# Gate rows from column products and a DRAM broadcast, value runs in single steps, the second key half summed on VectorE, transposes evacuated in pairs

## The chip, the core and the metric

The kernel runs on one core of one Trainium2 chip. Times are device microseconds; the time of the kernel before is the median of four runs, 1138.79 us (1138.46 to 1139.82). A profile is one execution, recorded by the hardware. It names TensorE "PE" (its weight loads "PEld"), VectorE "DVE", ScalarE "ACT", GpSimd "POOL" and SyncE "SP"; lines such as L960 are lines of the kernel's source.

## What is computed

One transformer block with adaptive layer norm, for 2048 tokens of width 1024, all in bf16:

```python
mod = (_silu(c) @ w_mod).reshape(c.shape[0], 6, 1, -1)
sa, ca, ga, sb, cb, gb = (mod[:, i] for i in range(6))
h = _layernorm(x) * (1 + ca) + sa
# 32 query heads of width 32, one key head and one value head (wk, wv: 1024 x 32)
q = h @ wq ; k = h @ wk ; v = h @ wv
p = softmax(q k^T / sqrt(32))            # per head, 2048 x 2048
x = x + ga * ((p v) @ wo)
h = _layernorm(x) * (1 + cb) + sb
x = x + gb * ((silu(h @ w1) * (h @ w3)) @ w2)     # w1, w3: 1024 x 3584
```

The vectors ga and gb ("gates") scale the columns of the attention's and of the MLP's output.

## The kernel before

**Who orders the work.** The program is written as a graph (class Dag). Every `G.add` names an engine, what the instruction reads and writes, an estimated duration and a priority. `schedule` runs through this graph with the estimates and fixes the order of the instructions on each engine; `emit` writes them in this order, with the waits that the data needs. An engine therefore works in the order found when the program was built, whatever the real durations are. At the places where several kinds of instruction could go next, `choose` may take another than the one the priorities prefer; the table CH (line 17) lists these decisions by the number of the choice. Two of the eight PSUM banks (PB0, PB1) go round among groups of matmuls; the other six (SP) hold scores during attention and join the round before and after.

**The head.** SyncE loads x, the first two parts of w_mod, and wq. The vector silu(c) lies as a column tile SCT (128 x 8). The first two modulation vectors are products of 128 x 128 weight tiles with single columns of SCT (L759), eight per load. LayerNorm statistics run on VectorE and for two tiles on ScalarE; TensorE transposes the normalized tiles (L624), and `ln_transpose` copies each transposed 128 x 512 piece out of PSUM, on ScalarE (L635) or VectorE (L638). Then follow the key projection (`kproj`, L674), the value projection (L690) and the query projection (`qproj`, L700), the last one for the first 256 tokens; the other query projections are filler for later.

**Attention.** It works on blocks of 256 queries, eight in all, and in each on eight groups f of four heads. One `step` takes two key tiles: eight score products (L960, four heads side by side), then two exps of 128 x 1024 on ScalarE (L970) into one of eleven U buffers. There are 64 steps per block, 512 in all. `finish` multiplies the U buffers of one f with V (L1026, 64 products of 256 columns, four heads side by side), in runs of two steps at a time. The sum of the exps over the keys (the softmax's denominator) is made in part by VectorE, which adds U buffers into a tree buffer (L987, L993; L1003 folds two of them), and then by products of the tree buffer with a selector of ones (L1053). The ratio is made from L1065, L1074, L1077 (evictions), L1083 (reciprocal), L1088 (spread) and L1093 (multiplication).

In block 0 the first four groups (HEAD = 4) run through the first half of the keys (h = 0) before the second half (h = 1), since later keys aren't projected yet. For the halves in DIRECT = (0, 1), that is both, VectorE makes no sum: four U buffers go straight to the selector products, 32 per half and group. L1062 adds the second half's result.

**After attention.** `post` does the output projection (L1158) with wo, whose columns were scaled by ga on VectorE (L895, 8 instructions), adds x (L1162), normalizes and transposes (through TensorE in the first and last block, with a transposing DMA, L1169, in the others). The MLP runs as 448 products of 256 columns for w1 and w3 (L1199) per block, tanh on ScalarE (L1207), three VectorE instructions (L1204, L1214, L1219), then the second layer (L1270, 224 products of 256 columns; L1241 in the last block). The MLP of one block is the filler between the score products of the next block. The weights w1, w3 and w2 come again for each block, through a ring of six buffers: three in WREG (behind WQ and the gates' weights), two in HREG, one in X.

**The gates before.** Four 128 x 4 x 512 pieces of w_mod per gate are loaded into three WMS slots. GpSimd spreads SCT into eight 128 x 128 tiles whose columns are all equal (SCB, L558). A product of such a tile with 512 columns of w_mod puts the gate's row on all 128 partitions at once (L884, sixteen products of 512 columns per gate), and L888 copies it into GBB, twice per gate. The modulation vectors 3 and 4 are made as in the head, by single columns (L910).

Of the kernel before, what the change touches and what calls it, by code (L numbers as in the profile page):

```python
# [16 lines left out]
CH = {88: 2, 187: 1, 188: 1, 196: 1, 205: 1, 224: 1, 229: 1, 262: 1, 329: 2, 352: 1, 362: 1, 375: 1, 411: 1,  # L17
      442: 1, 609: 2, 654: 2, 662: 1, 731: 1, 775: 1, 851: 2, 1272: 1, 1290: 2, 1463: 1, 1478: 1, 1492: 1, 1497: 1,
      1526: 1, 1897: 1, 1915: 2, 2088: 1, 2103: 1, 2117: 1, 2122: 1, 2151: 1, 2522: 1, 2540: 2, 2713: 1, 2728: 1,
      2742: 1, 2747: 1, 2776: 1, 3147: 1, 3165: 2, 3338: 1, 3353: 1, 3367: 1, 3372: 1, 3401: 1, 3772: 1, 3790: 2,  # L20
      3963: 1, 3978: 1, 3992: 1, 3997: 1, 4009: 1, 4163: 1, 4339: 1, 4342: 1, 4490: 1}
# [15 lines left out]
class Dag:  # L37
# [77 lines left out]
    def choose(self, t, e, n, alts):  # L115
        self.nch += 1
        return CH.get(self.nch - 1, 0)

# [295 lines left out]
def build(nc, x_in, wq_in, wk_in, wv_in, wo_in, w1_in, w3_in, w2_in, c_in, wmod_in, out, S, D, F):  # L414
# [41 lines left out]
    ACTP = -1  # L456
    TP = -1
# [9 lines left out]
    SCT = sb("SCT", [P, NC], BF16)  # L467
    CROW = sb("CROW", [8, P], BF16)
# [26 lines left out]
    DIRECT = (0, 1)  # L495
# [3 lines left out]
    SCB = [QT[:, k // 4, S - 512 + (k % 4) * P:S - 512 + (k % 4 + 1) * P] for k in range(NC)]  # L499
    WKV = QT[:, NC - 1, S - 512:S].rearrange("p (a c f) -> p a c f", a=2, c=NC)  # L500
    WKK, WVK = [("QT", NC - 1, S - 512), ("QT", NC - 1, S - 384)], [("QT", NC - 1, S - 256), ("QT", NC - 1, S - 128)]
    SCBK = [("QT", a, S - 512 + b) for a in range(NC // 4) for b in range(0, 512, P)]
# [14 lines left out]
    def grp(allow=None):  # L517
        g = Group()
        g.allow = allow
        return g  # L520
# [36 lines left out]
    for a in range(NC // 4):  # L557
        G.add("pool", lambda e, a=a: e.tensor_copy(  # L558
            QT[:, a, S - 512:S].rearrange("p (k q) -> p k q", q=P),
            SCT[:, a * 4:a * 4 + 4].unsqueeze(2).broadcast_to([P, 4, P])), reads=["SCT"],  # L560
            writes=[("QT", a, S - 512 + b) for b in range(0, 512, P)], dur=0.6)
# [52 lines left out]
    def ln_transpose(nt, q0, dst, dkeys, fs, fm, engs, prio=5, cbs=None, allow=None, bp=0):  # L614
# [3 lines left out]
        for cb in range(NC // ncb) if cbs is None else cbs:  # L618
            g = grp(allow)
            for i in range(nt):  # L620
                def tr(e, i=i, g=g, cb=cb):
                    for h in range(ncb):
                        c = cb * ncb + h
                        r = e.transpose(PBH[g.bank][:, h * w + i * P:h * w + (i + 1) * P],  # L624
                                        xnt(q0 + i)[:, c * P:(c + 1) * P], IDENT[:])
                    return r
                G.add("pe", tr, reads=["IDENT"] + [k for j in (range(nt) if i == 0 else (i,)) for k in [("XN", q0 + j)] + xnk(q0 + j)], dur=ncb * 0.065, lat=0.2,
                      acq=g if i == 0 else None, groups=[(g, "w")], mode="F", prio=prio)
            for h in range(ncb):
# [81 lines left out]
    ONPOOL = ()  # L711
    KP = 1
# [158 lines left out]
    def gate(m, scale):  # L871

        for h in range(2):
            g = grp()
            for kb in range(2):
# [6 lines left out]

                for k in range(4):
                    G.add("pe", lambda e, kb=kb, k=k, sl=sl, g=g: e.matmul(  # L884
                        PB[g.bank], SCB[kb * 4 + k], WMS[:, sl, k, :], start=(kb == 0 and k == 0),
                        stop=(kb == 1 and k == 3)), reads=SCBK + wms(sl), dur=MM, lat=0.2,
                        acq=g if kb == 0 and k == 0 else None, groups=[(g, "w")], mode="F")
            G.add("dve", lambda e, g=g, h=h: e.tensor_scalar(GBB[:, h * 512:(h + 1) * 512], PB[g.bank], scale, None,  # L888
                                                             ALU.mult),
                  writes=[("GBB", h)], groups=[(g, "r")], dur=dve_t(512), prio=4)  # L890

    G.chain = GCH
    gate(2, 1.0)
    for f in range(NC):
        G.add("dve", lambda e, f=f: e.tensor_tensor(WO[:, f, :], WO[:, f, :], GBB[:], ALU.mult),  # L895
              reads=["WO", ("GBB", 0), ("GBB", 1)], writes=[("WOG", f)], dur=dve_t(1024, 2), prio=6)
    for m in range(2):
        g = grp()
        for h in range(2):
            for kb in range(2):  # L900
                sl = nwm[0] % 3
                nwm[0] += 1
                c0 = (3 + m) * D + h * 512
                dma(lambda e, kb=kb, c0=c0, sl=sl: e.dma_start(
                    WMS[:, sl], wmod_in[kb * 512:(kb + 1) * 512, c0:c0 + 512].rearrange("(c p) f -> p c f", p=P)),
                    ("wms", sl), writes=wms(sl), nbytes=P * 2048 * 2)
# [10 lines left out]
        a, b2 = ((1.0, 0.0), (1.0, 1.0))[m]  # L917
        G.add("dve", lambda e, g=g, m=m, a=a, b2=b2: e.tensor_scalar(
            MODC[:, 3 + m, :], PB[g.bank][:, 0:8], a, b2, ALU.mult, ALU.add),
            writes=[("MODC", 3 + m)], groups=[(g, "r")], dur=0.15, prio=4)  # L920
    gate(5, 0.5)
# [9 lines left out]
    def attention(q0, qn):  # L931
# [65 lines left out]
        def finish(f, h=None):  # L997
# [21 lines left out]
            for w0 in range(0, nn, 2):  # L1019
                part = pend[w0:w0 + 2]  # L1020
# [43 lines left out]
            else:  # L1064
                G.add("dve", lambda e, g=g, f=f: e.tensor_copy(ASB[:, f % 4, 0:qn], PB[g.bank][:, 0:qn]),  # L1065
                      writes=[("ASB", f % 4), ("XN", 2 + f % 4 // 2)], groups=[(g, "r")], dur=dve_t(qn), prio=1)
# [5 lines left out]
            if ga not in opened:  # L1072
                opened.add(ga)
                G.add("dve", lambda e, g=g, da=da: e.tensor_copy(DSB[:, da, 0:qn], PB[g.bank][:, qn:2 * qn]),  # L1074
                      writes=[("DSB", da)], groups=[(g, "r")], dur=dve_t(qn), prio=1)
# [283 lines left out]
```

## Time and profile before

| | us |
|---|---|
| median of four runs | 1138.79 |
| the profiled execution | 1138.55 |
| its span | 1136.8 |
| ScalarE, 1024 exps (L970) | 960.9 busy, mean 1077 ns |
| ScalarE, 112 tanhs (L1207) | 75.0 busy |
| VectorE, sums of exps (L993, L987, L1003) | 291.6 + 146.1 + 63.3 busy |
| TensorE, 4096 score products (L960) | 203.4 busy |
| TensorE, 4096 value products (L1026) | 132.9 busy |
| TensorE, 800 selector products (L1053) | 32.5 busy |
| TensorE, 32 gate row products (L884) | 7.9 busy |

Busy time of a group is the union of its rows, in which instructions overlap: ends of matmuls are modelled, and the exps' rows reach into the next. How far apart two instructions start tells more than how long their rows are. The first exp starts at 27.4 us and the last at 1028.6 us. A row of the order of time gives start, length, engine, line, operation, output and input, count, and in brackets the idle time before it and what ended it.

### The profile page before, as it was taken

How to read it: one execution, taken by the hardware profiler on the slowest of the kernel's cores; microseconds unless marked ns; L12 is line 12 of the kernel's file. 1: busy time of each engine (PE TensorE's matmuls, PEld its weight loads, DVE VectorE, ACT ScalarE, POOL GpSimd, SP SyncE). 2: the span in 40 equal slices, each digit the busy share in tenths (PEclk: the TensorE clock that was granted, in tenths of full speed). 3: DMA queues.
4: the chain of work that ended last, by engine and by line, in shares of the span. 5: the costliest groups of instructions: out<-in, count | busy, mean ns of one | idle time of the engine just before them, and what ended most of it. 6: DMA issues, size and time to landing. Idle time of an engine off the chain costs nothing.

```text
span 1136.8 us, 35258 instructions
## 1 busy us (share of the span) xinstructions
PE 1111.8 (98%) x15678; PEld 745.2 (66%) x15711; DVE 986.2 (87%) x1501; ACT 1021.8 (90%) x1167; POOL 41.4 (4%) x86
## 2 busy tenths in 40 slices
PE   7999999999999999999999999999999999999998
PEld 4565344677667766777577756776677757777884
DVE  6838799999989998999989998999989999997552
ACT  5999999999999999999999999999999999992110
POOL 4200000000100001000100000000100000000000
PEclk9999999999999999999999999999999999999999
DMA  9616102975596567766587558765785649756994
GB/s 332 191 61 202 42 1 67 285 198 169 139 279 187 164 172 205 223 173 171 151 252 200 166 145 235 208 184 168 162 248 169 191 117 263 215 165 181 294 311 141
DMA packets 378536, 211.09 MB, mean 186 GB/s; under 512 B 21776, under 2 KB 369424, under 8 KB 378384
## 3 DMA queue, kind: packets, MB, share of 16 engines
q1 hardware_dynamic: 376304, 208.69, 65.7%
q8 instruction: 124, 2.03, 0.8%
q10 hardware_dynamic: 2080, 0.13, 0.1%
q14 instruction: 28, 0.23, 0.1%
HBM read 201.46 MB, written 4.19 MB: 181 GB/s over the span
## 4 chain that ended last, share of the span: by engine, by line
PE 82%; ACT 13%; DVE 1%; DMA 1%; SPq 1%; issue 1%; DVEq 0%
PE PB L1199 29%; PE PB L1270 14%; PE SP L960 12%; ACT UREG L970 12%; PE PB L1026 9%; PE PB L1158 4%; PE SP L1199 3%; PE PB L700 3%; PE SP L1270 2%; PE PB L1053 2%; PE PB L1241 1%; PE SP L1241 1%; DMA WREG<-in_B_w_dram 1%; DMA UREG<-in_w_mod_dram 1%; ACT WREG L1207 1%
## 5 line engine op out<-in xcount | busy, mean ns | idle before, releaser
L970 ACT ACTIVATE UREG<-SP 128x1024 bf16<-128x1024 f32 x1024 | 960.9, 1077 | 6.0 <-PE SP L960 4.3
L993 DVE TENSOR_TENSOR UREG<-UREG 128x2048 bf16<-128x2048 bf16 x240 | 291.6, 1215 | 7.6 <-ACT UREG L970 5.2
L960 PE MATMUL SP<-QT,KT 32*128 32x256 bf16 x4096 | 203.4, 273 | 6.1 <-ACT UREG L970 5.6
L1199 PE MATMUL PB<-QT,WREG 128*128 128x256 bf16 x1648 | 206.3, 273 | 1.0 <-DMA WREG<-in_B_w_dram 1.0
L1199 PEld LDWEIGHTS PB<-QT,WREG 128*128 128x128 bf16 x1648 | 150.3, 98 | 45.2 <-issue 28.1
L987 DVE TENSOR_TENSOR UREG<-UREG 128x2048 bf16<-128x2048 bf16 x120 | 146.1, 1218 | 9.4 <-ACT UREG L970 6.0
L960 PEld LDWEIGHTS SP<-QT,KT 32*128 32x128 bf16 x4096 | 60.7, 92 | 128.6 <-ACT UREG L970 69.4
L1026 PE MATMUL PB<-UREG,V 128*32 128x256 bf16 x4096 | 132.9, 274 | 1.5 <-ACT UREG L970 1.0
L1199 PE MATMUL PB<-QT,HREG 128*128 128x256 bf16 x1056 | 132.8, 273 | 0.0
L1026 PEld LDWEIGHTS PB<-UREG,V 128*32 128x32 bf16 x4096 | 98.8, 96 | 27.8 <-issue 19.4
L1207 ACT ACTIVATE WREG<-GSB 128x512 bf16<-128x512 bf16 x112 | 75.0, 670 | 45.1 <-DVE GSB L1204 45.1
L1199 PEld LDWEIGHTS PB<-QT,HREG 128*128 128x128 bf16 x1056 | 96.3, 98 | 27.9 <-issue 17.5
L1270 PE MATMUL PB<-WREG,HREG 128*128 128x256 bf16 x700 | 88.6, 273 | 0.2 <-issue 0.2
L1219 DVE SCALAR_TENSOR_TENSOR HREG<-WREG,HREG 128x512 bf16<-128x512 bf16 x112 | 75.8, 678 | 0.9
L1270 PEld LDWEIGHTS PB<-WREG,HREG 128*128 128x128 bf16 x700 | 64.0, 98 | 19.2 <-issue 11.8
L1204 DVE CAST GSB<-PB 128x512 bf16<-128x512 f32 x104 | 70.8, 680 | 4.1 <-PE PB L1199 3.2
L1214 DVE TENSOR_TENSOR HREG<-GSB,PB 128x512 bf16<-128x512 bf16 x98 | 66.3, 676 | 4.5 <-PE PB L1199 4.1
L1199 PE MATMUL PB<-QT,X 128*128 128x256 bf16 x528 | 67.5, 273 | 0.0
L700 PE MATMUL PB<-HREG,WREG 128*128 128x512 bf16 (+1 forms) x299 | 62.0, 338 | 2.4 <-issue 0.8
L1003 DVE TENSOR_TENSOR UREG<-UREG 128x2048 bf16<-128x2048 bf16 x52 | 63.3, 1217 | 0.2
L1270 PE MATMUL PB<-HREG 128*128 128x256 bf16 x476 | 61.2, 273 | 0.0
L1199 PEld LDWEIGHTS PB<-QT,X 128*128 128x128 bf16 x528 | 48.4, 98 | 13.7 <-issue 8.7
(144 smaller groups left out, 910.7 us busy)
## 6 DMA issues: line engine op xcount, KB each, us to landing
WREG<-in_B_w_dram SPq DMA_DIRECT2D x112, 512.0 KB, 5.6
HREG<-in_B_w_dram SPq DMA_DIRECT2D x74, 512.0 KB, 5.4
WREG<-in_B_w_dram SPq DMA_DIRECT2D x33, 896.0 KB, 5.2
X<-in_B_w_dram SPq DMA_DIRECT2D x38, 512.0 KB, 6.1
HREG<-in_B_w_dram SPq DMA_DIRECT2D x21, 896.0 KB, 5.3
X<-in_B_w_dram SPq DMA_DIRECT2D x10, 896.0 KB, 5.1
X<-in_A_x_dram SPq DMA_DIRECT2D x32, 256.0 KB, 5.4
WREG<-in_w_mod_dram SPq DMA_DIRECT2D x16, 512.0 KB, 5.1
```

Of the source, the lines that this page charges most:

```text
L700: g = mm_group(NC, lambda e, b, c: e.matmul(b[:, 0:n], WQ[:, c, f * P:(f + 1) * P], HT[:, c, sl], start=c == 0, stop=c == NC - 1), lambda ...
L960: r = e.matmul(SP[:, b, o:o + qn], KT[32 * gg:32 * gg + 32, kts[j] * P:(kts[j] + 1) * P], QT[32 * gg:32 * gg + 32, f, q0:q0 + qn], start=T ...
L970: G.add("act", lambda e, u=u, h0=h0, n=n, b0=b0, nb=nb: e.activation(U[:, u, h0 * W:(h0 + n) * W].rearrange("p (b w) -> p b w", b=nb), SP[ ...
L987: G.add("dve", lambda e, tr=tr, u=u, fu=first_u: e.tensor_tensor(TR[:, tr, 0:4 * W], U[:, fu, 0:4 * W], U[:, u, 0:4 * W], ALU.add), reads= ...
L993: G.add("dve", lambda e, tr=tr, u=u: e.tensor_tensor(TR[:, tr, 0:4 * W], TR[:, tr, 0:4 * W], U[:, u, 0:4 * W], ALU.add), reads=[("TR", tr) ...
L1026: r = e.matmul(PB[g.bank][32 * gg:32 * gg + 32, 0:qn], V[:, kt, :], U[:, pu, (gg * npk + j) * qn:(gg * npk + j + 1) * qn], start=w0 + n == ...
L1199: return e.matmul(bk[:, j * qn:(j + 1) * qn], w13[:, w, c, j * P:(j + 1) * P], QT[:, c, q0:q0 + qn], start=c == 0, stop=c == NC - 1)
L1204: G.add("dve", lambda e, g=g, b=b: e.tensor_copy(GS[b][:, 0:2 * qn], PB[g.bank][:, 0:2 * qn]), writes=[("GS", b)], groups=[(g, "r")], dur= ...
L1207: G.add("act", lambda e, b=b: e.activation(TB[b], GS[b], ACT.Tanh, scale=0.5), reads=[("GS", b)], writes=[("TB", b)], clear=alias("TB"), d ...
L1214: G.add("dve", lambda e, g=g, fp=fp, b=b: e.tensor_tensor(HHT[:, 2 * fp:2 * fp + 2, 0:qn], GS[b][:, 0:2 * qn].rearrange("p (j q) -> p j q" ...
L1219: G.add("dve", lambda e, fp=fp, b=b: e.scalar_tensor_tensor(HHT[:, 2 * fp:2 * fp + 2, 0:qn], TB[b][:, 0:2 * qn].rearrange("p (j q) -> p j ...
L1270: G.add("pe", lambda e, g=g, j=j, fc=fc, hf=hf, first=first, w2s=w2s: e.matmul(PB[g.bank][:, j * 256:(j + 1) * 256], HHT[:, hf * NH + fc, ...
```

## The change

- *Gates.* The new function `vec` makes any modulation vector by single columns (L890 in the changed kernel, 64 products per vector). `gate` calls it for the gate as a column tile GC (128 x 8), transposes GC on TensorE (8 x 128), copies it to GR, writes GR to a scratch row in DRAM (2 KB) and reads that row back onto all 128 partitions into GBB (256 KB). SCB and its two GpSimd copies are gone.
- *Second key half.* DIRECT is (0,): in the second half VectorE adds the four U buffers (three instructions per group, twelve in all), and 8 selector products take the place of 32 for each of the four groups.
- *Value runs.* The products with V are planned one step (8 products) at a time, where it were two steps.
- *Transposes.* With ME, a VectorE eviction of transposed tiles takes two 512-column pieces at once.
- *Planner.* EP gives the evictions of the last head group in each block an earlier priority; the table CH is new, and `choose` ignores an entry that names an alternative that isn't there.

```diff
-CH = {88: 2, 187: 1, 188: 1, 196: 1, 205: 1, 224: 1, 229: 1, 262: 1, 329: 2, 352: 1, 362: 1, 375: 1, 411: 1,
...
+CH = {2: 1, 3: 1, 63: 1, 136: 1, 138: 1, 147: 1, 161: 1, 176: 1, 187: 1, 223: 1, 237: 1, 244: 1, 249: 1, 263: 1,
...
-        return CH.get(self.nch - 1, 0)
+        c = CH.get(self.nch - 1, 0)
+        return c if c <= len(alts) else 0
...
+    EP = -3
...
+    GC = sb("GC", [P, 2, NC], BF16)
+    GR = sb("GR", [8, 2, P], BF16)
+    gscr = nc.dram_tensor("gscr", [2, D], BF16, kind="Internal").ap()
...
-    DIRECT = (0, 1)
+    DIRECT = (0,)
...
-    for a in range(NC // 4):
-        G.add("pool", lambda e, a=a: e.tensor_copy(
-            QT[:, a, S - 512:S].rearrange("p (k q) -> p k q", q=P),
-            SCT[:, a * 4:a * 4 + 4].unsqueeze(2).broadcast_to([P, 4, P])), reads=["SCT"],
-            writes=[("QT", a, S - 512 + b) for b in range(0, 512, P)], dur=0.6)
...
+            if ME and fs is None and engs[cb % len(engs)] == "dve":
+                c0, c1 = cb * ncb, (cb + 1) * ncb
+                G.add("dve", lambda e, g=g, c0=c0, c1=c1: e.tensor_copy(
+                    HT[:, c0:c1, q0 * P:q0 * P + w], PBH[g.bank].rearrange("p (c q) -> p c q", c=ncb)),
+                    writes=[k for c in range(c0, c1) for k in dkeys(c)], groups=[(g, "r")], dur=0.73, prio=1)
+                continue
...
-    def gate(m, scale):
-
+    def vec(m, key, out):
+        g = grp()
         for h in range(2):
-            g = grp()
...
-                for k in range(4):
-                    G.add("pe", lambda e, kb=kb, k=k, sl=sl, g=g: e.matmul(
-                        PB[g.bank], SCB[kb * 4 + k], WMS[:, sl, k, :], start=(kb == 0 and k == 0),
-                        stop=(kb == 1 and k == 3)), reads=SCBK + wms(sl), dur=MM, lat=0.2,
-                        acq=g if kb == 0 and k == 0 else None, groups=[(g, "w")], mode="F")
-            G.add("dve", lambda e, g=g, h=h: e.tensor_scalar(GBB[:, h * 512:(h + 1) * 512], PB[g.bank], scale, None,
-                                                             ALU.mult),
-                  writes=[("GBB", h)], groups=[(g, "r")], dur=dve_t(512), prio=4)
...
+    def gate(m):
+        i = m // 3
+        vec(m, ("GC", i), GC[:, i])
+        g = grp()
+        G.add("pe", lambda e, g=g, i=i: e.transpose(PBH[g.bank][0:8, 0:P], GC[:, i], IDENT[:]),
+              reads=["IDENT", ("GC", i)], dur=0.07, lat=0.2, acq=g, groups=[(g, "w")], mode="F")
+        G.add("dve", lambda e, g=g, i=i: e.tensor_copy(GR[:, i], PBH[g.bank][0:8, 0:P]), writes=[("GR", i)],
+              groups=[(g, "r")], dur=0.2, prio=0)
+        dma(lambda e, i=i: e.dma_start(gscr[i].rearrange("(k p) -> k p", p=P), GR[:, i]), ("gw", i), reads=[("GR", i)],
+            writes=[("GSCR", i)], nbytes=2048)
+        dma(lambda e, i=i: e.dma_start(GBB[:], gscr[i].unsqueeze(0).broadcast_to([P, D])), ("gr", i),
+            reads=[("GSCR", i)], writes=[("GBB", 0), ("GBB", 1)], nbytes=P * D * 2)
...
-            for w0 in range(0, nn, 2):
-                part = pend[w0:w0 + 2]
+            for w0 in range(0, nn, 1):
+                part = pend[w0:w0 + 1]
...
-                      writes=[("ASB", f % 4), ("XN", 2 + f % 4 // 2)], groups=[(g, "r")], dur=dve_t(qn), prio=1)
+                      writes=[("ASB", f % 4), ("XN", 2 + f % 4 // 2)], groups=[(g, "r")], dur=dve_t(qn), prio=EP if f == NC - 1 else 1)
```

## The prediction

> **What bounds the kernel now.** I read the page first, then busy times by stretch, then TensorE in order of time.
>
> ```profile
> PE 1111.8 (98%) x15678; PEld 745.2 (66%) x15711; DVE 986.2 (87%) x1501; ACT 1021.8 (90%) x1167; POOL 41.4 (4%) x86
> ```
>
> ```profile
> 60.00:80.00 20.00, 19.91 (x442) 13.65 (x431) 7.72 (x18) 19.75 (x22) 0.00 (x0) 1.00 0.10 31
> 80.00:100.00 20.00, 19.69 (x310) 10.99 (x309) 15.18 (x30) 19.80 (x23) 0.00 (x0) 1.00 0.35 107
> ...
> 180.00:200.00 20.00, 16.91 (x282) 8.74 (x281) 19.96 (x29) 20.00 (x23) 0.00 (x0) 1.00 0.42 110
> ...
> 525.30:651.10 125.80, 125.59 (x1800) 85.54 (x1801) 117.19 (x171) 125.29 (x143) 3.44 (x4) 1.00 0.68 190
> ```
>
> The columns after the length are TensorE, weight loads, VectorE, ScalarE, GpSimd. From 60 to 1028 us ScalarE (the exps) never rests, and from 200 us on TensorE doesn't either. The stretches need different sums, so I priced TensorE's work from the last blocks:
>
> ```profile
> 1015.31 1.93 PE L1026 MATMUL PB<-UREG,V 128*32 128x256 bf16 x64
> 1017.07 0.39 PE L1053 MATMUL PB<-UREG,SEL 128*32 128x256 bf16 x8
> 1017.39 0.40 PE L960 MATMUL SP<-QT,KT 32*128 32x256 bf16 x8
> 1017.72 1.59 PE L1199 MATMUL PB<-QT,WREG 128*128 128x256 bf16 x13
> 1019.25 0.40 PE L960 MATMUL SP<-QT,KT 32*128 32x256 bf16 x8
> ```
>
> Starts tell the price, ends are modelled. 13 products of 256 columns take 1019.25 - 1017.72 = 1.53 us, 13 x 0.109 and 0.11 for leaving their mode; 64 value products 1.76, 64 x 0.0274 (four run side by side) and the same 0.11; eight score products 0.33, again 0.0274 each and 0.11. So every change between the three modes (score, value or selector, full) costs TensorE about 0.107 us. One middle block holds 512 score, 512 value, 72 selector products at 0.0274, 672 MLP products at 0.109, 32 output products at 0.2165 (1.62 us for seven in the chain, with the change) and 142 mode changes: 30.0 + 73.2 + 6.9 + 15.2 = 125.4. The same step of two blocks starts at 524.84 and 650.61: 125.77. TensorE leaves 0.4 us per block. ScalarE needs 128 exps x 0.916 (starts) + 14 tanhs x 0.52 = 124.5.
>
> Here the Trainium skill speaks against any gain. "Perfetto Trace Analysis", section "Identifying the Most-Contended Engine", calls matmul busy time a bad measure and judges TensorE by weight-load busy share. That is 85.54 of 125.80, 68%: a third of TensorE would be free, ScalarE would bind, and cheaper TensorE work would be worth 0. The row sum gives the full difference. I take the sum: it adds up to the block's length within 0.3%, and the mode changes are in neither busy share.
>
> **The change, part by part.** I number score groups 0 to 511 ("steps"). The issue order of both built programs is fixed, so I counted in it.
>
> *Value runs in single steps, with the new table of choices.* Between step 97 and step 511 the old order has 909 mode changes, the new one 887: 22 x 0.107 = -2.4 us. In the same stretch the new order issues 22 MLP products fewer, 14 because they already ran before step 97 and 8 because they are left for the end: 22 x 0.109 = -2.4. TensorE's sum falls from 814.4 to 809.6. The trace needs 817.0 (step 97 starts at 210.17, step 511 at 1027.21), 2.6 above the sum; as TensorE comes closer to ScalarE's own need (828 exps x 0.916 + 95 tanhs x 0.52 = 808), I let the idle grow by 1 (bounds 0 and 4): -3.8 (-4.8 to -0.8).
>
> *The tail.* After step 511 the order keeps everything but 210 instead of 202 second-layer products (L1270). TensorE runs without a pause there, so 8 x 0.109 = +0.9. The priority of the last head group's evictions moves VectorE work behind 58 products of cover (56 before): 0; without that cover one eviction, 0.42.
>
> *Second key half on VectorE, block 0.* Four times 32 selector products become 8: 96 x 0.0274 = -2.6 us of TensorE, but in the stretch where ScalarE sets the pace (1.83 us per step, two exps).
>
> ```profile
> 61.41 1.06 PE L1026 MATMUL PB<-UREG,V 128*32 128x256 bf16 x32
> 62.30 1.05 PE L1053 MATMUL PB<-UREG,SEL 128*32 128x256 bf16 x32
> 63.27 0.40 PE L960 MATMUL SP<-QT,KT 32*128 32x256 bf16 x8
> ```
>
> A step with 32 + 32 lasts 63.27 - 61.08 = 2.19, 0.36 too long for the exps. Exps are late by 4.0 in all at step 92 (172.4 for 92 x 1.83), of which such steps gave about 1.1, the crowded step at 39 us 0.5, and the first step 0.8. The new order spreads these; its own long steps (2.01 at 34, 37 and 40) follow short ones and give perhaps 0.6; its first step starts 0.3 later because 16 more key products stand ahead. Net -1.7 at step 86. The price is on VectorE: 12 sums of 1.215 (row of L993) = +14.6. VectorE idles 23.8 us between 60 and 140 us (12.3 of them from 60 to 80), which hides it. If not, what is queued behind the sums are the Q evictions (0.74 each), and for them waits TensorE with its two free banks.
>
> *Gates.* Removed: 32 row products (7 in 1.62, as for any 512 columns: 6.9 us), four evictions of 0.68 (2.7), two GpSimd copies (1.2 us, before the first exp and beside other work: 0). Added: 128 column products, 2 transposes, four tiny VectorE copies (0.15 to 0.2: 0.7), four DMAs on SP's queue. The nearest row is L910, the same form:
>
> ```profile
> 98.74 0.95 PE L910 MATMUL PB<-SCT,WREG 128*128 128x1 bf16 x32
> ```
>
> The next full product starts at 99.77, so 32 take 1.0: 0.031 each, 128 = 4.0. Again a rule speaks against it: "TensorE: Matmul & The Clock Gate", section "LDWEIGHTS (loading the stationary operand)", says that a load takes its columns over 1.2 in ns, 107 ns for 128 columns, whatever is streamed (the page's fast weight load about halves it). By it the 128 products cost an estimated 13.7 us, 6.8 more than the rows, and steps with 36 to 44 of them would hold the exps up by some 5. I take the trace's 0.031: -2.9 net, in steps that mostly have room, so 0 on the path.
> The DRAM detour has no row. Write and read back lie between two of the quickest landings (128 KB out, 1.8 each: 3.6 us) and 2.4 (the 2 KB of c are used that long after issue) + 5.4 (256 KB of x, median) = 7.8. The read is issued behind three more weight loads, at about 102 us, and lands at 104 to 108; VectorE takes the WO products up at about 106, so it may stand for 0 to 2 us, with 6.7 of idle between 100 and 140 beside it and WO wanted only at 160: 0. SP's later loads stand behind both detours, but wait for the last Q products at 188 us anyway.
>
> *Transposes in pairs.* 20 copies at 0.375 (0.75 for two, starts) become 10 of 0.6 to 0.8 on VectorE: -1.5 to +0.5, ahead of step 16 with other work beside: 0.
>
> *MLP start.* This is what the head hands on.
>
> ```profile
> 191.32 6.88 SPq L1189 DMA_DIRECT2D WREG<-in_B_w_dram  x5
> ...
> 198.81 0.40 PE L960 MATMUL SP<-QT,KT 32*128 32x256 bf16 x8 [0.46 <-ACT UREG L970]
> 200.25 1.59 PE L1199 MATMUL PB<-QT,WREG 128*128 128x256 bf16 x13 [1.04 <-DMA WREG<-in_B_w_dram]
> ```
>
> The weights load when the last Q product is done; the second group needs the third transfer, 8.9 after the first issue. The new order ends the Q products one step earlier (86, not 87). With the 1.7 that is 191.3 - 1.8 - 1.7 = 187.8, and the third transfer lands at 196.7. The product that needs it stands in step 91, at 195.8, so 1 us is waited again. Steps 92 to 96 add 10.6, and step 97 starts at 208.6 instead of 210.2: -1.6. For VectorE's added load I take -1.0 (-1.6 to +1.5).
>
> *Sum:* -1.0 - 3.8 + 0.9 = -3.9: span 1136.8 - 3.9 = 1132.9; with the 1.75 around it in the profiled execution (1138.55) 1134.65, and that execution lies 0.24 under the median: **1134.9 us**, 0.34% faster.
>
> **Rivals.** (1) *ScalarE is the bound after all*, as the weight-load share has it: exps slip as before and what TensorE saves becomes idle. For it: 99.6% busy. Against it: its busy rows overlap (mean 1077 ns, starts 916 apart), and 124.5 is under 125.8. It takes 2 to 4 of the 3.8: 1137 to 1139, no measurable change.
> (2) *VectorE holds up the MLP start: slower.* Place: 140 to 200 us, where VectorE has 1.1 us of idle in 60. If the 12 sums aren't done by 140, Q evictions, the first residual add and LN come late by what is left. While the MLP waits TensorE can do only attention, 0.7 of each 1.83 (scores and values 0.33 each with their mode changes), so 1 us late costs 0.6. It decides from 6.5 us late (0.6 x 6.5 eats 3.9); all 12 late give +7.4 - 3.9: 1142. Against it: idle of 23.8 before.
> (3) *The column products cost a full weight load:* +5 in steps 30 to 51: about 1140. Against it the row above.
>
> **How the numbers follow.** This kernel's runs scatter so that about 0.2% (2.3 us) is what can be told from no change. The sum: 0.67, and its own range is 1132.3 to 1136.5; rival 1: 0.21; rivals 2 and 3, and a wait I haven't found: 0.12. Faster 0.67, same 0.21, slower 0.12. The low end takes the best of both main terms (-1.6 - 4.8 + 0.9); the high end reaches through rival 1 to 1139.0 and leaves out the slower cases.
>
> **What would show it.** Right: steps of neighbouring middle blocks 125.0 to 125.4 apart; selector products 704; step 97 at 208.5 to 209.5 and step 511 near 1022.5; column products about 1.0 per 32. Wrong: blocks still 125.7 apart with TensorE waiting for exps (rival 1); step 97 after 212 with VectorE full before 140 (rival 2); a VectorE stop of several us at the WO products.

## The result, and the profile after

The changed kernel takes 1137.63 us (median of 34 runs, 1135.14 to 1140.77), the kernel before 1138.92 us, measured beside it (52 runs): a ratio of 0.9987, 95% interval 0.9982 to 0.9992. It is faster, by 0.13%. The forecast was 1134.9 us and 0.34%. The time lies inside the stated range, but above 1136.5, where the range of the prediction's own sum ended; and the gain is smaller than the 0.2% that the prediction called the limit of what can be told. The profiled execution took 1137.62 us, its span 1135.8.

The busy line of the page, which answers the first one shown of the kernel before:

```profile
PE 1110.4 (98%) x15685; PEld 746.4 (66%) x15716; DVE 996.6 (88%) x1503; ACT 1021.2 (90%) x1167; POOL 40.4 (4%) x84
```

VectorE has 10.4 us more (986.2 before), TensorE 1.4 less. This does not show where the time went. The starts of the score groups do ("steps", as in the prediction, eight L960 products each):

| start of | before, us | after, us | difference | predicted |
|---|---|---|---|---|
| first exp | 27.41 | 28.81 | +1.40 | +0.3 |
| step 36 | 94.52 | 94.93 | +0.41 | |
| step 40 | 102.02 | 103.41 | +1.39 | |
| step 44 | 109.53 | 110.74 | +1.21 | |
| step 52 | 124.12 | 126.01 | +1.89 | |
| step 56 | 131.91 | 135.33 | +3.42 | |
| step 86 | 187.98 | 190.90 | +2.92 | -1.7 |
| step 97 | 210.17 | 212.59 | +2.42 | -1.0 |
| step 511 | 1027.21 | 1025.41 | -1.80 | -4.8 |
| end of span | 1136.75 | 1135.82 | -0.94 | -3.9 |

From step 97 to 511 the kernel gained 4.22 us (3.8 forecast), and the tail lost 0.87 (0.9 forecast). All that is missing was lost before step 97, and most of it in three short places between 94 and 136 us. Busy times by stretch of the changed kernel; after the length stand TensorE, weight loads, VectorE, ScalarE, GpSimd, then the granted TensorE clock:

```profile
60.00:80.00 20.00, 19.48 (x369) 13.20 (x366) 15.10 (x24) 19.93 (x23) 0.00 (x0) 1.00 0.03 8
80.00:100.00 20.00, 17.78 (x325) 10.03 (x326) 15.89 (x23) 20.00 (x24) 0.00 (x0) 0.98 0.42 123
95.73:99.14 3.41, 2.61 (x67) 1.88 (x69) 3.41 (x7) 3.41 (x5) 0.00 (x0) 1.00 0.13 20
99.14:102.56 3.42, 3.14 (x15) 0.76 (x13) 2.59 (x6) 2.28 (x4) 0.00 (x0) 0.50 0.93 266
102.56:112.80 10.24, 8.73 (x194) 5.10 (x196) 10.09 (x18) 10.24 (x12) 0.00 (x0) 1.00 0.65 213
112.80:116.21 3.41, 3.41 (x38) 1.43 (x31) 3.00 (x6) 2.91 (x4) 0.00 (x0) 0.50 0.74 244
116.21:126.45 10.24, 8.05 (x192) 4.93 (x193) 10.17 (x16) 10.24 (x12) 0.00 (x0) 1.00 0.33 104
126.45:129.87 3.42, 3.42 (x16) 0.72 (x16) 2.19 (x3) 2.26 (x3) 0.00 (x0) 0.50 0.00 1
180.00:200.00 20.00, 18.21 (x293) 9.34 (x292) 19.89 (x29) 19.99 (x23) 0.57 (x1) 1.00 0.35 90
525.56:650.76 125.20, 124.99 (x1799) 85.85 (x1801) 117.11 (x171) 125.15 (x143) 3.35 (x4) 1.00 0.69 190
```

Three times, for 3.41 us each, the granted clock is 0.50 (a "dip" from here on), and ScalarE works only 2.28, 2.91 and 2.26 us of 3.4. In the profiled execution of the kernel before, the clock stayed at 1.00 from 8.2 us to the end of the program, and ScalarE did not rest in these stretches. The first of them in the kernel before:

```profile
99.14:102.56 3.42, 3.25 (x61) 1.63 (x59) 3.42 (x6) 3.42 (x4) 0.00 (x0) 1.00 0.65 180
```

The last row of the changed kernel's stretches is a middle block, 125.20 us long (125.77 before). TensorE in order of time around the first dip:

```profile
97.08 1.25 PE L890 MATMUL PB<-SCT,WREG 128*128 128x1 bf16 x44
98.50 0.40 PE L960 MATMUL SP<-QT,KT 32*128 32x256 bf16 x8 [0.17 <-ACT UREG L970]
98.83 2.90 PE L705 MATMUL PB<-HREG,WREG 128*128 128x512 bf16 x7
101.67 0.61 PE L960 MATMUL SP<-QT,KT 32*128 32x256 bf16 x8
```

The 44 column products took 1.25 us, no more than forecast (44 x 0.031 = 1.36). They are of vector 3, as the order of `vec` and the evictions (L898) show; the kernel before makes vectors 3 and 4 by single columns too (L910), the gates are what is new. The seven Q products behind them took 2.90; in the kernel before the same seven take 1.68 or 1.69:

```profile
96.80 1.69 PE L700 MATMUL PB<-HREG,WREG 128*128 128x512 bf16 x7
...
98.74 0.95 PE L910 MATMUL PB<-SCT,WREG 128*128 128x1 bf16 x32
99.77 0.38 PE L700 MATMUL PB<-HREG,WREG 128*128 128x512 bf16 x1
```

So the next score group came late (101.67), and ScalarE stood. The other two dips, at 112.8 and 126.5 us, follow column products of vector 4 and of the second gate, and slow what comes behind them in the same way.

The first exp, 1.40 us late, has another cause. TensorE in order of time in the kernel before, around its first score group:

```profile
26.38 0.40 PE L960 MATMUL SP<-QT,KT 32*128 32x256 bf16 x8
26.71 0.40 PE L674 MATMUL PB<-HREG,WKS 128*32 128x512 bf16 x4
28.14 1.48 PE L674 MATMUL PB<-HREG,WKS 128*32 128x512 bf16 x24 [1.03 <-issue]
```

and in the changed kernel:

```profile
25.75 0.84 PE L679 MATMUL PB<-HREG,WKS 128*32 128x512 bf16 x12
28.03 0.40 PE L679 MATMUL PB<-HREG,WKS 128*32 128x512 bf16 x4 [1.45 <-issue]
28.37 0.40 PE L960 MATMUL SP<-QT,KT 32*128 32x256 bf16 x8
```

Both stop for over a microsecond, waiting for nothing that the profile shows ("issue"). Counting TensorE's records, products and weight loads together, both stop after the 700th. Before, that was behind the first score group; now 16 products of 512 columns stand ahead of the group, and the stop is ahead of it too.

### The profile page after: what moved, and what is told of

It is laid out like the page before. It is cut to its first block, busy times and chain, and to the rows that moved or that the text cites. A ratio compares the mean times of both kernels' runs of the same rounds, so it can differ in the third digit from the quotient of the medians.

```text
span 1135.8 us, 35265 instructions
## 1 busy us (share of the span) xinstructions
PE 1110.4 (98%) x15685; PEld 746.4 (66%) x15716; DVE 996.6 (88%) x1503; ACT 1021.2 (90%) x1167; POOL 40.4 (4%) x84
## 4 chain that ended last, share of the span: by engine, by line
PE 87%; ACT 9%; DVE 2%; POOL 1%; issue 0%; DMA 0%; SPq 0%; DVEq 0%
PE PB L1199 33%; PE PB L1270 14%; PE SP L960 13%; ACT UREG L970 9%; PE PB L1026 9%; PE PB L1158 4%; PE SP L1199 3%; PE PB L705 2%; PE SP L1270 2%; PE PB L1053 1%; PE SP L1241 1%; PE PB L1241 1%; PE SP L1158 1%; DVE UREG L987 1%; DVE UREG L1003 0%
## 5 line engine op out<-in xcount | busy, mean ns | idle before, releaser
L993 DVE TENSOR_TENSOR UREG<-UREG 128x2048 bf16<-128x2048 bf16 x248 | 301.3, 1215 | 3.4 <-ACT UREG L970 1.4
L960 PE MATMUL SP<-QT,KT 32*128 32x256 bf16 x4096 | 204.1, 274 | 6.0 <-ACT UREG L970 5.2
L987 DVE TENSOR_TENSOR UREG<-UREG 128x2048 bf16<-128x2048 bf16 x124 | 150.9, 1217 | 15.3 <-ACT UREG L970 15.3
L960 PEld LDWEIGHTS SP<-QT,KT 32*128 32x128 bf16 x4096 | 60.8, 92 | 127.6 <-ACT UREG L970 78.2
L1207 ACT ACTIVATE WREG<-GSB 128x512 bf16<-128x512 bf16 x112 | 80.3, 717 | 45.8 <-DVE GSB L1204 45.8
L705 PE MATMUL PB<-HREG,WREG 128*128 128x512 bf16 (+1 forms) x298 | 65.1, 351 | 3.7 <-DVE QT L708 1.2
L1199 PE MATMUL PB<-QT,X 128*128 128x256 bf16 x512 | 65.0, 273 | 0.0
L1003 DVE TENSOR_TENSOR UREG<-UREG 128x2048 bf16<-128x2048 bf16 x52 | 63.3, 1217 | 0.0
```

Of the source, the lines that this page charges most:

```text
L705: g = mm_group(NC, lambda e, b, c: e.matmul(b[:, 0:n], WQ[:, c, f * P:(f + 1) * P], HT[:, c, sl], start=c == 0, stop=c == NC - 1), lambda ...
L960: r = e.matmul(SP[:, b, o:o + qn], KT[32 * gg:32 * gg + 32, kts[j] * P:(kts[j] + 1) * P], QT[32 * gg:32 * gg + 32, f, q0:q0 + qn], start=T ...
L987: G.add("dve", lambda e, tr=tr, u=u, fu=first_u: e.tensor_tensor(TR[:, tr, 0:4 * W], U[:, fu, 0:4 * W], U[:, u, 0:4 * W], ALU.add), reads= ...
L993: G.add("dve", lambda e, tr=tr, u=u: e.tensor_tensor(TR[:, tr, 0:4 * W], TR[:, tr, 0:4 * W], U[:, u, 0:4 * W], ALU.add), reads=[("TR", tr) ...
L1199: return e.matmul(bk[:, j * qn:(j + 1) * qn], w13[:, w, c, j * P:(j + 1) * P], QT[:, c, q0:q0 + qn], start=c == 0, stop=c == NC - 1)
L1207: G.add("act", lambda e, b=b: e.activation(TB[b], GS[b], ACT.Tanh, scale=0.5), reads=[("GS", b)], writes=[("TB", b)], clear=alias("TB"), d ...
```

## The experiments

My theory from these rows: one-column products keep TensorE's row busy but hardly move data through the array; this counts as rest, and the granted clock is halved for a whole window of 3.41 us. The rivals: the clock falls for another reason (a wait, the new order), VectorE's 12 added sums hold up the first block, or ScalarE and not TensorE binds the blocks.

**Column products that keep the array busy.** Each streams its one column 64 times; order and plan are the changed kernel's. The edit stands in `vec`, so it widens all 256 products of the four vectors, not the gates' 128 alone.

```diff
-  e.matmul(PB[g.bank][:, h * 4 + j:h * 4 + j + 1], WMS[:, sl, k, j * P:(j + 1) * P],
-           SCT[:, kb * 4 + k:kb * 4 + k + 1],
+  e.matmul(PB[g.bank][:, (h * 4 + j) * 64:(h * 4 + j + 1) * 64], WMS[:, sl, k, j * P:(j + 1) * P],
+           SCT[:, kb * 4 + k:kb * 4 + k + 1].broadcast_to([P, 64]),
...
-  e.tensor_scalar(out, PB[g.bank][:, 0:8], a, b2, ALU.mult, ALU.add)
+  e.tensor_scalar(out, PB[g.bank][:, 0:8 * 64].rearrange("p (j n) -> p j n", n=64)[:, :, 0], a, b2, ALU.mult, ALU.add)
```

> The changed kernel, but each of the 128 column products streams its one column 64 times (64 equal output columns, the eviction reads every 64th). Same plan, same order, 128 x 63 more columns for TensorE. My theory: in the changed kernel the granted TensorE clock fell to 0.5 three times for 3.41 us (at 99.1, 112.8, 126.5 us) because the one-column products leave the array idle, and this pushed step 97 from about 209.7 to 212.59. With 64 columns the clock stays at 1.00 from 9 us to the end, step 97 starts at 209.4 to 210.2 (2.4 to 3.2 earlier), the later spans stay as they are, and the profiled time falls from 1137.6 to about 1134.8 to 1135.4; the median about 1135.3, 0.3% under the kernel before. Rival (the clock's fall has another cause, such as the pause at 110 to 112 us while the score group waits, or step 97 is late through VectorE's added sums): the dips stay or step 97 stays at 212 to 213, and the time stays at 1137.6, or rises by up to 1 us because the products are longer.

Measured: 1135.45 us against 1139.81, ratio 0.9966 (0.9952 to 0.9979), granted clock 1.00 in all five runs. In its profile (span 1132.3) step 97 starts at 209.07, which is 3.52 earlier than in the changed kernel; from there to step 511 it needs 812.83 us, the changed kernel 812.82. The whole difference of the two spans is made before step 97; at step 36, ahead of the dips, it is only 0.21. TensorE in order of time at the first of the three places:

```profile
96.81 1.54 PE L890 MATMUL PB<-SCT,WREG 128*128 128x64 bf16 x44
98.19 0.38 PE L705 MATMUL PB<-HREG,WREG 128*128 128x512 bf16 x1
98.50 0.40 PE L960 MATMUL SP<-QT,KT 32*128 32x256 bf16 x8
98.83 1.68 PE L705 MATMUL PB<-HREG,WREG 128*128 128x512 bf16 x7
100.45 0.40 PE L960 MATMUL SP<-QT,KT 32*128 32x256 bf16 x8
```

The 44 products take 98.19 - 96.81 = 1.38 us; the seven Q products are back at 1.68. By their own starts the 44 lie 0.031 us apart, where those of one column lay 0.025 apart (1.35 and 1.09 us from the first to the last). So the 63 extra columns cost 0.006 us each time, an estimated 1.5 us of TensorE for the 256, and hold the clock.

**The same with 8 columns** (64 replaced by 8 in that diff).

> As the 64-column version, with 8 equal columns instead of 64. If the clock goes by how much the array streams, 8 columns (under a tenth of the product's 31 ns period at full rate, by the 256 columns in 0.109 us of this kernel: 3.4 ns) are still too few: one to three dips of 3.41 us, step 97 at 211 to 212.6, time 1136 to 1137.6. If any product of more than one column counts, it equals the 64-column version: no dip, step 97 at 209.4 to 210.2. Rival (the number of columns has nothing to do with it): equals the changed kernel, 212.6 and 1137.6, and so does the 64-column version.

Measured: 1137.56 us, ratio 0.9983 (0.9974 to 0.9992), granted clock 0.995 to 0.998 in all ten runs. Its profile has two dips, with step 97 at 211.21:

```profile
110.23:113.64 3.41, 3.27 (x15) 0.93 (x16) 3.02 (x5) 2.69 (x4) 0.00 (x0) 0.50 1.03 350
120.47:123.89 3.42, 3.42 (x71) 2.09 (x60) 3.04 (x3) 2.76 (x5) 0.00 (x0) 0.50 0.51 158
```

So it is not enough that a product has more than one column; the clock goes with how many are streamed.

**The kernel before with thin rows.** The reverse test: the 32 row products of the gates stream 8 columns instead of 512, so 504 of 512 columns of the gate rows are left out; the order and the sizes of VectorE's work are those of the kernel before.

```diff
-  PB[g.bank], SCB[kb * 4 + k], WMS[:, sl, k, :], start=(kb == 0 and k == 0),
+  PB[g.bank][:, 0:8], SCB[kb * 4 + k], WMS[:, sl, k, 0:8], start=(kb == 0 and k == 0),
...
-  e.tensor_scalar(GBB[:, h * 512:(h + 1) * 512], PB[g.bank], scale, None, ALU.mult)
+  e.tensor_scalar(GBB[:, h * 512:(h + 1) * 512], PB[g.bank][:, 0:1].broadcast_to([P, 512]), scale, None, ALU.mult)
```

> The kernel before, with its 32 row products of the two gates streaming 8 columns instead of 512; all else as before (it leaves out 504 of 512 columns of the gate rows; the evictions write as many columns, all from one). If it is what the array streams that holds the clock, the kernel before now shows the dips of the changed one: one to three of 3.41 us between 95 and 135 us, step 97 at 211 to 213 instead of 210.17, time 1139.5 to 1141. Rival (another part of the change makes the clock fall, such as VectorE's added sums or the new order): clock stays at 1.00, step 97 at 209.5 to 210.3, time 1137.5 to 1138.6.

Measured: 1140.31 us against 1139.02, ratio 1.0009 (1.0000 to 1.0018), clock 0.995 to 0.998 in eight runs of ten. The kernel before falls below 1.00 by itself, in 7 of the 18 runs beside these, but never below 0.998; here five of ten lie at 0.995 to 0.997. In the profile there is one dip, and step 97 starts at 211.47:

```profile
127.23:130.64 3.41, 3.24 (x15) 0.88 (x15) 2.66 (x4) 3.10 (x4) 0.00 (x0) 0.50 0.00 0
```

TensorE was given less to do, and the kernel did not become faster: neither the new order nor the added sums are needed for the dips.

**The first score group ahead of the 16 key products**, on top of the 64 columns.

```diff
+ pe = order["pe"]
+ z = next(i for i, n in enumerate(pe) if n.cls == "S")
+ a = z
+ while pe[a - 1].mode == "V" and pe[a - 1].dur > 0.2:
+     a -= 1
...
+ pe[a:z + 1] = [pe[z]] + pe[a:z]
```

> As the 64-column version, and the first score group is moved ahead of the 16 key products of 512 columns in TensorE's order. My theory: TensorE stops 1.4 to 1.9 us at its 705th instruction (counting products and loads of weights as recorded), whatever that is; in the kernel before this stood behind the first score group, in the changed one ahead of it. With the group moved forward it stands behind it again: first exp at 28.2 to 28.4 instead of 28.8 (no earlier, as ScalarE scales the weights until 28.2), and 0.2 to 0.6 us off the time of the 64-column version. Rival (the stop is tied to the time of about 26 to 28 us or to the key products' data, not to the count): the first group waits wherever it stands, first exp at 28.8, same time as the 64-column version.

Measured: 1134.84 us, ratio 0.9960 (0.9948 to 0.9973), not to be told from the 64-column version (1135.45; the intervals overlap). In the profile the first exp starts at 27.94 (28.2 to 28.4 expected; the 64-column version has 28.25), and the stop stands behind the first group, after record 699. This profiled execution took 1136.52 with one dip, at 27.65 us, in which the moved key products ran at half clock (step 1 at 31.86 instead of 29.79); the other four runs had a clock of 1.00 and took 1134.17 to 1135.23.

**The kernel before with 15 TensorE products more ahead of the first group:** 15 warm-up products of 512 columns split in two.

```diff
-  for _ in range(k):
-      r = e.matmul(PB[b], IDENT[:], IDENT[:].unsqueeze(1).broadcast_to([P, 4, P]), start=True, stop=True, skip_group_check=True)
+  m = 2 if k == 15 else 1
+  for _ in range(k * m):
+      r = e.matmul(PB[b][:, 0:512 // m], IDENT[:], IDENT[:].unsqueeze(1).broadcast_to([P, 4 // m, P]), start=True, stop=True, skip_group_check=True)
```

> The kernel before, with 15 of its warm-up products of 512 columns split into 30 of 256 columns, so that TensorE has 15 products and 15 loads of weights more ahead of the first score group, with the same columns streamed. My theory (TensorE stops at its 705th instruction): the stop of 1.0 to 1.4 us now falls ahead of or inside the first score group, and the first exp starts at 28.0 to 28.8 instead of 27.4; the time is 0.3 to 1.2 us longer. Rival (the stop belongs to the time or to the work that stands there): the stop stays where it was, behind the first score group, first exp at 27.3 to 27.5, and the time is that of the kernel before.

Measured: the first exp moved from 27.41 to 28.39. TensorE in order of time:

```profile
25.46 1.05 PE L674 MATMUL SP<-HREG,WKS 128*32 128x256 bf16 x29
27.72 0.29 PE L674 MATMUL SP<-HREG,WKS 128*32 128x256 bf16 x3 [1.21 <-issue]
27.94 0.40 PE L960 MATMUL SP<-QT,KT 32*128 32x256 bf16 x8
```

The same work ran at the same time up to 25.5 us, but the stop now cuts it after record 701, ahead of the score group. It goes with the count: in the twelve traces it begins at 25.7 to 27.1 us, but always after record 699 to 701. But the time did not grow: 1138.88, ratio 0.9999 (0.9990 to 1.0008). By step 1 only 0.34 of the 0.98 was left, because the key products that used to be cut were now not, and 0.18 at step 97. That part of my expectation was wrong: the stop costs about the same on either side of the first group.

**Both together:** the first group moved, and 12 warm-up products split so that the stop meets a wait for keys.

```diff
+  for n in range(k):
+      m = 2 if k == 15 and n < 12 else 1
+      for _ in range(m):
+          r = e.matmul(PB[b][:, 0:512 // m], IDENT[:], IDENT[:].unsqueeze(1).broadcast_to([P, 4 // m, P]), start=True, stop=True, skip_group_check=True)
```

> As the version with the first score group moved forward, and 12 of the warm-up products of 512 columns split into 24 of 256 columns: 24 more recorded TensorE instructions (12 products, 12 loads of weights) ahead of the first score group. My theory: TensorE's stop goes by the count of instructions (699 to 701 by record in five kernels so far), so it now falls at the gap of 1.25 us in which TensorE waits for the first keys anyway (instruction 676, 25.4 to 26.6 us): no stop behind the first score group, second score group at 28.8 to 29.3 instead of 29.8, and the time 0.3 to 0.9 us under the 64-column version (about 1134.4 where that has 1135.3). Rival (the stop belongs to the time of 26 to 28 us): it stays behind the first score group and nothing is gained.

Measured: the stop fell exactly there (after record 700, just ahead of the first score group), but the group started at 27.32 instead of 26.67 and the second at 30.17, not 28.8 to 29.3. The time was 1136.09, ratio 0.9973 (0.9963 to 0.9984): no gain. Where the stop is to be put to cost nothing I have not found.

**The 64-column version again**, measured beside the last one.

> The 64-column version once more, beside the one with the stop moved. My theory: clock at 1.00 in all or nearly all runs, median 1135.2 to 1135.6, ratio to the kernel before 0.9965 to 0.9975. Rival (its earlier lead was the luck of five runs): 1136 to 1138 with a granted clock below 1.00 in some runs.

Measured: 1134.72 us, ratio 0.9965 (0.9952 to 0.9977), clock 1.00 in all five runs. This is the version to keep: 0.35% under the kernel before, and by the two ratios (0.9965 and 0.9987) 0.2% under the changed one.

**28 products more per block**, on the 64-column version; one product of each first-layer group counts double.

```diff
-  return e.matmul(bk[:, j * qn:(j + 1) * qn], w13[:, w, c, j * P:(j + 1) * P], QT[:, c, q0:q0 + qn], start=c == 0, stop=c == NC - 1)
+  for n in range(2 if i == 3 else 1):
+      r = e.matmul(bk[:, j * qn:(j + 1) * qn], w13[:, w, c, j * P:(j + 1) * P], QT[:, c, q0:q0 + qn], start=c == 0, stop=c == NC - 1)
+  return r
```

> The 64-column version, with one of the 16 products of each group of the MLP's first layer issued twice (its product counts double in the sum): 28 products more per block, 28 x 0.109 = 3.05 us of TensorE; ScalarE's work unchanged. If TensorE sets the pace of the blocks, as predicted: middle blocks go from 125.2 to 128.1 to 128.4 (+2.9 to +3.2), from step 97 to step 511 +20 to +21, time about +24 in all (1159.5). Rival (ScalarE sets the pace, and TensorE has slack in it): the blocks take up the slack first and grow by less than 2.6, time less than +20.

Measured, a middle block:

```profile
532.51:660.66 128.15, 127.94 (x1827) 88.60 (x1829) 117.55 (x171) 127.33 (x143) 3.35 (x4) 1.00 0.68 187
```

125.20 became 128.15: +2.95 for 3.05 us of TensorE. Step 97 to 511 grew by 20.08 us, the time is 1159.62 (a single run). TensorE sets the pace of the blocks, with 0.1 us of slack in each.

**A lighter first layer:** 4 of 16 products stream 32 of 256 columns, so 7/8 of a quarter of that layer is left out.

```diff
-  return e.matmul(bk[:, j * qn:(j + 1) * qn], w13[:, w, c, j * P:(j + 1) * P], QT[:, c, q0:q0 + qn],
+  m = 32 if c in (2, 5) else qn
+  return e.matmul(bk[:, j * qn:j * qn + m], w13[:, w, c, j * P:(j + 1) * P], QT[:, c, q0:q0 + m],
```

> The 64-column version, with 4 of the 16 products of each group of the MLP's first layer streaming 32 of 256 columns (it leaves out 7/8 of a quarter of that layer): 112 products per block, each 0.06 to 0.078 shorter, 6.7 to 8.7 us of TensorE per block. If TensorE sets the pace now and ScalarE stands close behind (128 exps x 0.916 + 14 tanhs x 0.52 = 124.5): middle blocks fall from 125.2 to 124.5 to 124.9 and no further, step 97 to step 511 by 2 to 5; the tail, where TensorE runs alone, by 4 to 7. Rival (ScalarE sets the pace already): blocks stay at 125.2, only the tail falls. Third (ScalarE's need is lower than I sum it): blocks fall to 117 to 121.

Measured in a single run (1131.77 us), a middle block:

```profile
522.68:647.73 125.05, 118.01 (x1802) 78.66 (x1803) 116.97 (x171) 125.00 (x143) 3.35 (x4) 1.00 0.70 191
```

TensorE is busy 7.2 us less, and the block is only 0.15 shorter: ScalarE's own need is 125.05 (busy 125.00), not the 124.5 that I summed. From step 97 to 511 the gain is 1.07, not 2 to 5. The tail became 2.2 shorter, not 4 to 7. There TensorE, now early, waits 2.89 us (up to 1098.79 us) for the second layer's weights, and behind this wait, at 1099 us, stands a dip of 3.41 us, worth up to 1.7. With both added the gain would be 5.1 to 6.8.

**Shorter sums on VectorE:** eight of the twelve added sums, those on L993 for the first four groups of heads, run over 128 of 2048 columns (15/16 of each is left out), on the 64-column version. The four sums on L987 stay.

```diff
+  hw = W // 4 if q0 == 0 and f < HEAD else 4 * W
...
-  TR[:, tr, 0:4 * W], TR[:, tr, 0:4 * W], U[:, u, 0:4 * W], ALU.add),
+  TR[:, tr, 0:hw], TR[:, tr, 0:hw], U[:, u, 0:hw], ALU.add),
```

> The 64-column version, with the second-half sums of block 0's first four heads over 128 of 2048 columns in both key halves (it leaves out 15/16 of these sums): 8 VectorE instructions of about 1.2 us become short, about 8 to 9 us off VectorE ahead of 140 us. My theory (VectorE's added sums are hidden): step 97 within 0.3 of the 64-column version's 209.07, time unchanged. Rival (VectorE holds up the start of the MLP or the exps of the first block): step 97 earlier by 0.5 to 4.

Measured: 1136.38 us in a single run, step 97 at 211.28, so later than 209.07, not earlier. Neither number that was expected came. But from step 20 to step 91 it took 131.20 us, the 64-column version 131.30 and 131.19: within 0.1 us the eight sums are hidden. The 2.2 came at two other places: 1.0 between steps 16 and 20, with two stops of 0.20 and 0.54 "issue" on TensorE, and 1.4 at step 91, where it waits for the MLP's weights:

```profile
199.39 1.38 PE L1200 MATMUL PB<-QT,WREG 128*128 128x256 bf16 x11 [1.21 <-DMA WREG<-in_B_w_dram]
```

This wait stands in the profiles of four versions with the 64 columns (0.85, 1.11, 1.16, 1.21 us) and not in the other three; part of what these versions scatter by is in it.

## Why the prediction was right and wrong

The number fell into the range by luck. The range reached beyond 1136.5 us only for rival 1, in which ScalarE turns TensorE's saving into idle time. This did not happen: the blocks gained all that was forecast, and the time was lost in the head, for a reason that the prediction names nowhere.

**Right: the blocks.** Step 97 to 511: -3.8 forecast, -4.22 measured; middle blocks 125.20 apart (125.0 to 125.4 forecast); 704 selector products; and the doubled products show that TensorE's sum is what the blocks follow. The weight-load busy share, which the prediction weighed and put aside ("Perfetto Trace Analysis", section "Identifying the Most-Contended Engine"), is 69% in a block whose length follows TensorE product by product; the measurement decides against it here. It is one of two measures that the section names; the other, the share of the peak FLOPs, the prediction did not work out.

**Right: the tail**, +0.87 for 8 products of 0.109.

**Wrong: the head.** Step 97 was to start 1.0 us earlier and started 2.42 later. The step that failed is "-2.9 net, in steps that mostly have room, so 0 on the path" for the gates. Its price for the products themselves was not too low (0.031 each; by their own starts 0.025), and rival 3, a full weight load per product, is refuted. What is wrong is that the price of a column product was taken to be its own duration only. Where products of one column stand close together the array streams little; the clock fell to 0.50 for three windows, and the work behind paid: step 36 to 40 +0.98, 44 to 52 +0.68, 52 to 56 +1.53, together 3.19. The 64-column version, with the same order and no dip, starts step 97 3.52 and 3.15 us earlier in two profiles. How much of this is the gates' own is open: only the third dip follows gate columns (the thin rows of the kernel before bring one dip at the same place), the first two follow those of vectors 3 and 4, which the new order places anew, and no run widened the gates' 128 alone.

The prediction used the page "TensorE: Matmul & The Clock Gate" for the weight loads; its section "Part 1: The HAM clock gate (the "warmup" mystery)" says that the throttled state is the default, and that activity in a free-running window of about 3.4 us releases it. The length agrees with the dips (3.41 us). But the section's word for a fall is an idle window, and TensorE's row was busy 2.61 of 3.41 us before the first dip: by the rule alone the clock could have been expected to hold. I read the granted clock in the rows of the kernel before, 1.00 in each, and did not ask which work held it there.

**Mis-sized: the first steps.** "0.3 later" was 1.40 in the changed kernel and 0.84 in the 64-column version. The 0.56 between them are not the clock's: the same key products start at 25.75 and 25.21 us, both at a clock of 1.00. The term left out for the first exp is the stop behind the 700th record, which I had in the trace of the kernel before as 1.03 us of "issue" and took for part of that kernel's own start. But it costs little further on: at step 1 the 64-column version is only 0.24 behind the kernel before. Step 3 is 1.40 behind, because it starts 2.64 us after step 2 (1.75 before): the new order puts 24 value-projection products (L695) there instead of 16, and TensorE stops once more for 0.56 us of "issue" at 34.0 us. The prediction had no term for this.

With the clock held, step 97 comes 1.10 and 0.74 us earlier than before in two profiles, where I had 1.0. This agreement is partly luck as well. Step 86 comes 0.60 and 0.24 earlier, not 1.7: that is the loss in the first steps. From step 86 to 97 both gain 0.50, where my -1.7 and -1.0 allowed a loss of 0.7 for VectorE.

**Half right: rival 1.** ScalarE does not bind the kernel before, but its floor is 125.05 and not 124.5 per block. Of the 0.72 us that a block had above it, the change took 0.57. More TensorE work saved there is worth 0.15 at most.

**Not seen: rival 2.** Its sign, step 97 after 212, came (212.59), but from the clock: with 64 columns, and the same sums, it starts at 209.07. VectorE still idled 13.8 us between 60 and 140 us, and the shortened sums move nothing. The gates' detour through DRAM was costed at nothing, and no cost shows: the WO products (L917) start at 111.48, not at about 106, but without a wait for a transfer.

**The bound of 0.2%.** Part of the scatter is the number of dips. Over the 34 runs of the changed kernel the mean time is 1136.15 us at a granted clock of 0.998 (3 runs), 1137.15 at 0.997 (12) and 1138.15 at 0.995 (14); one, two and three windows of 3.41 us at half clock would be 0.0015, 0.003 and 0.0045 of the span. Its single run at 1.00 took 1135.43. But the runs at 0.997 still differ by 2.5 us, and the ten runs with 64 columns, all at 1.00, reach from 1134.18 to 1136.71. In the kernel before, beside the first 64-column test, ten runs at 1.00 took 1138.10 to 1138.93 and the other eleven 1139.81 to 1140.72; in the later set of 18 the two kinds overlap.

**Sums and readings of the prediction that do not hold.** The 1.76 us of the value row are 64 x 0.0274 alone; selector products follow in the same mode, and the 0.11 for the change stands in the selector row (0.32). The mode changes do lie inside TensorE's busy row: it is busy 125.59 of 125.80 us, and products alone sum to 110. And the low end's own terms (-1.6 - 4.8 + 0.9 from 1138.79) give 1133.3, not 1132.3. None of these moves the forecast.

Left open: the change was not split further. No run had only the new table of value runs, or only the pairs of transposes; that the 22 mode changes and 22 moved products make up the 4.22 follows from the sum and from the doubled products, not from a run of their own.

## What to carry to other kernels

Before replacing wide products by many narrow ones, ask of each stretch of 3.4 us how much the array still streams, not how busy TensorE's row is. Where it gets thin, widening the narrow products costs little (here 64 columns at 0.031 us each instead of one at 0.025) and can hold the clock. Look at the granted clock of the changed kernel before any other view, and at its value in every run when a kernel's times scatter. And an "issue" stop early in a trace can go with a count of instructions, as here: work put ahead of the first important group can carry the stop ahead of it as well.

## What the runs showed of the hardware

- **A busy row does not hold the clock; what is streamed does.** This can be estimated for each window of 3.41 us on the grid of the next point: every product counts its columns x 0.109/256 us, one on a quarter of the array a quarter of that. From 12 us on the twelve traces have 3939 such windows at full clock. The 20 after which the clock fell, 8 inside the program and 12 at its end, streamed 0.00 to 0.35 of their length; all others streamed 0.38 or more. Before the three dips of the changed kernel it is 0.22, 0.32 and 0.25, before those of the 8-column version 0.27 and 0.34, before that of the thin rows 0.35, with the first group moved 0.31, and in the tail of the lighter first layer, where TensorE waits, 0.10. TensorE's busy row does not part the two kinds: it was busy 2.61 of 3.41 us before the first dip, and in 70 windows in which it was busy no longer than that the clock stayed.
- **Dips start on a grid.** The three of the changed kernel begin 13.66 and 13.65 us apart, four times 3.41, and each lasts one such length. In each of the twelve traces the first rise of the clock, its dips and its fall at the end lie on one such grid. Where it lies differs from trace to trace (the first rise stands at 8.0 to 11.2 us), which fits that one kernel dips in some of its runs and not in others.
- **TensorE stops at a count.** After 699 to 701 records (products and loads) each of the twelve traces has a stop: 1.07 to 1.83 us between two starts, 0.86 with the first group moved. Split warm-up products move it to other work at the same count.
- **The stops follow transfers on an instruction queue.** The page of every run lists a queue q8 of the kind "instruction" (number, MB, share; the line below). Its 124 transfers (125 in one run) have 16 KB each, one for some 253 of TensorE's 31,400 records. In the twelve traces TensorE has 21 stops of over 0.4 us put down to "issue". Each ends 1.2 to 1.6 us after such a transfer has landed: among them the stop at record 700 in eleven traces, the one at 34.0 us and the one of 0.54 us with shortened sums. So a late supply of instructions is the likely cause; no run moved a transfer to show it.

```profile
q8 instruction: 124, 2.03, 0.8%
```
